# The last stage of an attention and two-MLP kernel written in a fixed order on every engine, with the rooms of its first inputs moved

## The chip, the cores and the metric

The kernel runs on one core of a Trainium2 chip. The metric is the device time of one execution in microseconds (us): the median of several runs. In this text PE is the matrix engine (TensorE) and PEld its weight loads, DVE the VectorE, ACT the ScalarE, POOL the GpSimd, and SP the engine that issues nearly all transfers.

## The reference

Attention over 4 sequences of 576 positions with 8 heads of 64, half of them with a local window of 32, half with a stride of 32; then one MLP with a product, then a second with a gelu. All is in float32.

```python
x = attn_out.transpose(0, 2, 1, 3).reshape(2304, 512)
y = (((x @ w1) * (x @ w2)) @ w3) @ moe_w_out       # 512 -> 1024 -> 512
h = y @ w_in                                       # 512 -> 2048
g = h * (1.0 / (1.0 + np.exp(-1.702 * h)))
return g @ w_out                                   # 2048 -> 512
```

## The kernel before

**Arithmetic.** Every float32 factor is split in a high part (ACT, `split_hi`, L246) and a low part (DVE, `split_lo`, L252: the rest). A product of two factors is three matmuls: high by low, low by high, high by high (`ORDER`). The weights arrive as 64-bit words that ACT and DVE turn into float32 first: two ACT conversions (L1137, L1138) and three DVE steps (L1139 to L1141). The products of the second MLP go by a scheme with seven products for a 2 by 2 block product, so each weight unit is turned into seven combinations of 256 columns.

**Stages.** Three lists of steps are written ahead of the last stage, `steps1`, two called `steps2`, and `steps3`. Each step has a time in units of 12 matmuls of 288 columns, and `written` sorts a list and issues it in that order on PE, DVE, ACT and SP. The batches of attention and of the first MLP run in them. Beside that work the weights of the second MLP are prepared:

- `u_placed`: eight units of `w_in` are converted and stored to `widram` (stage `steps2`; times `UNITS_2`).
- `wo_steps`: eight units of `w_out` are converted, summed into seven combinations, split and stored to `tdram`, high parts by `store(0)` and low parts by `store(1)`. Unit 0 is early (`EARLY_AT`, in the second `steps2`, rooms in pool `cv`). Units 1 to 6 are in `steps3` (`UNIT` apart), unit 7 is late, in the last stage.

`steps3` is the last batch. Its first 8 units (-8 to 0) are the end of the batch before: `y_products` (L1166) with their copies `ysb` (L1174), which go to `ydram`. From 0 on come `pieces(3, hb, m)` (L715): per m two products of 12 matmuls, a copy on ACT (`abf`, L1226), a multiplication on DVE (L1229), and a split into `ab` (L246, L252), and `fourth` (L1350), the last product of the first MLP. Beside it stand `y_load` (L1290), which reads the first 768 rows of y back from `ydram`, and `y_steps` (L1308, L246, L252), which forms seven combinations of y and splits them into `yq`. `y_load(0, 0)` goes into the tile `raw` of pool `cv_a`, `y_load(0, 1)` into that of `cv_b`; the rooms of `steps3` (pools on the right side of the memory) come to lie where pools of the earlier stages lay.

**The last stage** (second MLP) runs over 3 blocks of 768 rows. A block has 8 quads and then 5 sweeps. A quad (`quad`) takes one unit of `w_in`, `hl`: seven products of six matmuls with 384 columns (`product`, L1461) into three PSUM tiles x, y, z, with copies of x and z by ACT (`keep`, L1474: s1, u1, z1), additions by DVE (L1467), gelu by ACT (L1453), differences by DVE (L1470), and a split of two of the results (`split`, tile `sp`). The five results of a quad stay in `parts[i]`. Between the products of quad i stand two pieces (`piece`, L1483: nine matmuls with 256 columns) of quad i - 1. A sweep is eight pieces, one for each `parts[i]`. The pieces read `tdram` factors from a ring of eight rooms (`t_more`, L1442). The factors of a quad come by `w_fetch` (L1327) and are split by `w_split`. The fetch of quad n is issued in quad n - 2, into the tile `x` of `cv_a`.

Unlike the stages before it, this last one isn't written by times: a planner (the scheduler of the tile framework, which reorders instructions of one engine by its own costs) decides the order on each engine. On PE it also takes pieces apart: a few matmuls of one stand between those of a product.

## Time and profile before

| | us |
|---|---|
| median of 3 runs | 818.17 (815.62 to 819.21) |
| the profiled execution, its own time | 817.43 |
| its span, first to last instruction | 815.6 |
| PE busy, share of the span | 780.1, 96% |
| PEld busy | 750.5, 92% |
| DVE busy | 585.6, 72% |
| ACT busy | 484.8, 59% |

Times in the rows are microseconds from the start of the span. An instruction's row has its start, its duration, engine, line, the tiles it writes and reads, their sizes, and in brackets the idle time of the engine before it with what ended that. A row of the timeline may merge several instructions of one kind (x30). The ends of matmuls are modelled, so a bracket on PE leaves out a part of each gap; the distance between starts has all of it. The chain follows the work that ended last back from the end. The last stage begins on PE at about 442 us; 337 to 379 us is the passage from the third to the last batch of the first MLP.

### The profile page before, as it was taken

To read this page: it belongs to the slowest core of one execution; us is meant where nothing else is said; L and a number is where in the kernel's file an instruction comes from. 1 tells how busy PE (TensorE), PEld (TensorE's weight loads), DVE (VectorE), ACT (ScalarE), POOL (GpSimd) and SP (SyncE) were. 2 spreads that over 40 slices of the span, in tenths; PEclk is the share of its full clock that TensorE was granted. 3 is DMA by queue.
4 is the path that set the end of the run, shared out by engine and by line. 5 is a ranking of instruction groups with operands and counts; after the bars stand their busy time and mean duration, and the time that the engine had idled before them with its cause. 6 is when DMAs were issued, how large, how long until landed. Compare 5 with 4: busy or idle time off the path is not lost.

```text
span 815.6 us, 16751 instructions
## 1 busy us (share of the span) xinstructions
PE 780.1 (96%) x6545; PEld 750.5 (92%) x6545; DVE 585.6 (72%) x1248; ACT 484.8 (59%) x1040; POOL 5.8 (1%) x14
## 2 busy tenths in 40 slices
PE   5899999999999999879999998999999999999997
PEld 4889999978999999878999898999999999999997
DVE  4889678788787787837776786885576885667653
ACT  6857655576665464425546665864566764666553
POOL 2000000000000000000000000000000000000000
PEclk9999999999999999989999999999999999999999
DMA  8976555541887553177899876499344489344472
GB/s 264 301 283 235 176 174 179 181 146 39 289 269 264 165 211 129 59 218 222 239 279 296 309 194 227 168 327 333 129 145 154 167 275 314 112 160 147 134 249 83
DMA packets 72063, 168.14 MB, mean 206 GB/s; under 512 B 6321, under 2 KB 45233, under 8 KB 69425
## 3 DMA queue, kind: packets, MB, share of 16 engines
q1 hardware_dynamic: 71840, 167.04, 62.2%
q8 instruction: 51, 0.84, 0.4%
q14 instruction: 28, 0.22, 0.1%
q10 hardware_dynamic: 144, 0.04, 0.0%
HBM read 130.88 MB, written 36.18 MB: 205 GB/s over the span
## 4 chain that ended last, share of the span: by engine, by line
PE 72%; DMA 11%; DVE 8%; ACT 6%; issue 1%; SPq 0%; ACTq 0%; DVEq 0%
PE acc L1483 21%; PE ps L715 18%; PE ps L1461 17%; PE ps L1166 8%; PE acc L1018 3%; DMA x<-widram 2%; PE acc L1350 2%; ACT hl L246 1%; PE sc L532 1%; DMA raw<-in_w 1%; DMA rawx<-in_w 1%; DVE hl L252 1%; DMA tdram<-sums 1%; PE pv L601 1%; DMA abdram<-abf 1%
## 5 line engine op out<-in xcount | busy, mean ns | idle before, releaser
L1483 PE MATMUL acc<-w,sp 128*128 128x256 f32 x1512 | 190.2, 283 | 1.4 <-DVE sp L252 1.1
L1483 PEld LDWEIGHTS acc<-w,sp 128*128 128x128 f32 x1512 | 187.1, 191 | 3.4 <-ACT sp L246 1.7
L1461 PE MATMUL ps<-yq,hl 128*128 128x384 f32 x924 | 171.1, 337 | 3.7 <-ACT s L1474 3.7
L1461 PEld LDWEIGHTS ps<-yq,hl 128*128 128x128 f32 x924 | 158.0, 188 | 7.4 <-ACT s L1474 7.1
L252 DVE TENSOR_TENSOR sp<-part,sp 128x384 fp32r<-128x384 f32 x144 | 77.8, 556 | 54.0 <-ACT sp L246 53.3
L715 PE MATMUL ps<-xah,w 128*128 128x288 f32 x512 | 104.1, 298 | 0.0
L715 PE MATMUL ps<-xbh,w 128*128 128x288 f32 x512 | 102.6, 295 | 0.7 <-DVE w L252 0.7
L246 ACT ACTIVATE sp<-part 128x384 fp32r<-128x384 f32 x144 | 73.7, 525 | 44.9 <-PE acc L1483 43.5
L715 PE MATMUL ps<-xal,w 128*128 128x288 f32 x256 | 77.8, 304 | 7.7 <-ACT ysb L1174 5.1
L1166 PE MATMUL ps<-ab,w 128*128 128x288 f32 x576 | 81.3, 301 | 2.7 <-DVE ab L252 2.6
L715 PEld LDWEIGHTS ps<-xah,w 128*128 128x128 f32 x512 | 83.6, 191 | 0.0
L715 PEld LDWEIGHTS ps<-xbh,w 128*128 128x128 f32 x512 | 81.9, 188 | 1.2 <-DVE w L252 1.2
L1166 PEld LDWEIGHTS ps<-ab,w 128*128 128x128 f32 x576 | 78.8, 191 | 3.8 <-DVE ab L252 2.9
L715 PE MATMUL ps<-xbl,w 128*128 128x288 f32 x256 | 77.2, 301 | 1.7 <-ACT abf L917 1.3
L1453 ACT ACTIVATE part<-part 128x384 f32<-128x384 f32 x72 | 37.3, 524 | 41.3 <-DVE part L1467 40.8
L246 ACT ACTIVATE ab<-abf 128x288 fp32r<-128x288 f32 x64 | 27.6, 440 | 55.3 <-DVE abf L1229 47.6
L715 PEld LDWEIGHTS ps<-xal,w 128*128 128x128 f32 x256 | 49.0, 191 | 9.9 <-ACT ysb L1174 5.7
L252 DVE TENSOR_TENSOR hl<-x,hl 128x1792 fp32r<-128x1792 f32 x21 | 42.5, 2025 | 16.2 <-ACT hl L246 16.1
L715 PEld LDWEIGHTS ps<-xbl,w 128*128 128x128 f32 x256 | 48.0, 188 | 3.2 <-ACT abf L917 1.5
L1018 PE MATMUL acc<-w,w 128*128 128x512 f32 x192 | 45.8, 398 | 0.1
L1470 DVE TENSOR_TENSOR part<-part 128x768 f32<-128x768 f32 (+1 forms) x48 | 36.3, 757 | 11.9 <-ACT part L1453 11.2
L1018 PEld LDWEIGHTS acc<-w,w 128*128 128x128 f32 x192 | 35.9, 188 | 9.3 <-ACT raw L1024 0.8
(180 smaller groups left out, 1079.0 us busy)
## 6 DMA issues: line engine op xcount, KB each, us to landing
w<-tdram SPq DMA_DIRECT2D x84, 512.0 KB, 5.3
x<-widram SPq DMA_DIRECT2D x21, 896.0 KB, 4.6
raw<-in_win SPq DMA_DIRECT2D x8, 1024.0 KB, 5.3
widram<-x SPq DMA_DIRECT2D x8, 896.0 KB, 5.4
raw<-in_wout SPq DMA_DIRECT2D x6, 1024.0 KB, 6.2
tdram<-raw SPq DMA_DIRECT2D x6, 896.0 KB, 5.3
tdram<-sums SPq DMA_DIRECT2D x6, 896.0 KB
raw<-in_w3t SPq DMA_DIRECT2D x10, 512.0 KB, 4.8
```

The source lines that it names most:

```text
L246: nc.scalar.activation(hi, src, AF.Copy)
L252: e.tensor_tensor(lo, src, r(hi), op=ALU.subtract)
L532: nc.tensor.matmul(sc[:nq, g, i * P:i * P + nk], qs[rows, i], ks[rows, i], start=True, stop=True,)
L601: nc.tensor.matmul(pv[rows, h // 2, :nq], L["v"][:nk, h * D:(h + 1) * D], ps[:nk, h * nq:(h + 1) * nq], start=True, stop=True,)
L715: nc.tensor.matmul(ps, ws[a][m // 2][:, at:at + P], xh[c][:, k, cols], start=(k == 0 and (a, c) == ORDER[0]), stop=(k == KC - 1 and (a, c) ...
L1018: nc.tensor.matmul(acc[f], hl[:, a, f * P:(f + 1) * P], wor[c][g], start=(g == 0 and (a, c) == ORDER[0]), stop=(g == MC - 1 and (a, c) == ...
L1166: nc.tensor.matmul(yacc[n], wfs[a][k][:, n * P:(n + 1) * P], hold[s % 2, k][:, c], start=(k == 0 and (a, c) == ORDER[0]), stop=(k == MC - ...
L1350: nc.tensor.matmul(st[0], wfs[a][k][:, n * P:(n + 1) * P], hold[hb, k][:, c], start=(k == 0 and (a, c) == ORDER[0]), stop=(k == MC - 1 and ...
L1453: nc.scalar.activation(dst, src, AF.Gelu_apprx_sigmoid)
L1461: nc.tensor.matmul(ps, w[a][:, f * 256 + kk * P:f * 256 + (kk + 1) * P], yq[:, b, kk, c], start=(first and kk == 0 and (a, c) == ORDER[0]) ...
L1470: nc.vector.tensor_tensor(dst, x, y, op=ALU.subtract)
L1483: nc.tensor.matmul(to, g[:, a, t * P:(t + 1) * P], t3[:, i % 2, c], start=(opens and i == 0 and n == 0 and t % 2 == 0), stop=(i == NU - 1 ...
```

## The change

- The last stage is written as the others are, in a list `steps4` with times in us (`do`), so the order on PE, DVE, ACT and SP is fixed. A product counts 1.05, a piece 1.07, a quad 9.49. `Quad`, `Split`, `Factors`, `Out` and `after` hold the steps. The arithmetic is the same.
- In the last quad of a block the piece of its first result stands ahead of its last product, and the piece of its last result stands behind the first two pieces of the first sweep. Copies and additions of the accumulators are placed one by one.
- The factors of quads 2 and 3 are fetched at the stage's start into the low half of their own split tiles; later ones three quads ahead, by turns into the tiles `x` and `raw` of `cv_a`. The split of the factors is cut: high part, first 1024 columns of the low part, the rest. A block's first factors are split in the sweeps before it.
- The late unit of `w_out` is spread over quads 1 to 5, and its high part goes to `parts[6]` and not to the raw room.
- Pool `cv_a` is opened ahead of `yc`, so both lie elsewhere on the right side.
- In the stages before: unit 7 of `w_in` one unit of time earlier, the early unit of `w_out` 2.2 earlier, the y steps and the units of `w_out` of the last batch 0.8 later, and the units 7.2 instead of 7.3 apart.

The diff, cut to its core (helpers that only change their names, and the copies and additions of the accumulators, are left out):

```diff
--- before.py
+++ after.py
...
-UNITS_2 = ((4, 6.4), (5, 15.6), (6, 24.2), (7, 32.8))
+UNITS_2 = ((4, 6.4), (5, 15.6), (6, 24.2), (7, 31.8))
...
-EARLY_AT = 37.8
+EARLY_AT = 35.6
...
-    def wo_steps(u, raw, room):
+    def wo_steps(u, raw, room, high_room=None):
         view = lambda t: raw().bitcast(t).rearrange("p (n t) -> p n t", t=2)
-        hi = lambda: raw().bitcast(F32R)[:, :7 * 256]
+        hi = lambda: (high_room or raw)().bitcast(F32R)[:, :7 * 256]
...
+    cv_a = pool("cva", stack=right1, side="right")
     yc = pool("yc", stack=right1, side="right")
-    cv_a = pool("cva", stack=right1, side="right")
     cv_b = pool("cvb", stack=right2, side="right")
...
-    def w_fetch(n, room=None):
+    def w_fetch(n, room):
         if n < NB * NU:
-            if room is not None:
-                x = room
-            elif n == 2:
-                x = p2.tile([P, 2, 7 * 256], F32, tag="hl", name="lent")[:, 0]
-            else:
-                x = cv_a.tile([P, 2 * CW2], F32, tag="x", name="x")[:, 256:]
-            nc.sync.dma_start(x, widram[n % NU])
-            wq[n] = x
...
-    def w_split(n):
-        if n < NB * NU:
-            t = (p2 if n % 2 else cv_a).tile([P, 2, 7 * 256], F32R, tag="hl", name="hl")
-            split_hi(t[:, 0], wq[n])
-            split_lo(t[:, 1], wq[n], t[:, 0])
-            wq[n] = t[:, 0], t[:, 1]
...
+            nc.sync.dma_start(room, widram[n % NU])
+            wq[n] = room
...
-    for kk, at in ((0, -4.4), (1, -1.2)):
+    for kk, at in ((0, -3.6), (1, -0.4)):
...
-    UNIT = 7.3
+    UNIT = 7.2
     for u in range(1, NU):
-        at = 1.8 + UNIT * (u - 1)
-        steps3.append((-1.4 if u == 1 else 1.55 + 0.1 * u if u < 4 else at - 2 * UNIT + 0.2, lambda u=u: wo_load(u)))
+        at = 2.6 + UNIT * (u - 1)
+        steps3.append((-0.6 if u == 1 else 2.35 + 0.1 * u if u < 4 else at - 2 * UNIT + 0.2, lambda u=u: wo_load(u)))
         if u < NU - 1:
             steps3 += [(at + g, f) for g, f in wo_steps(u, lambda u=u: todo3[u], lambda u=u: sums[:, u % 2])]
...
-    def t_more():
-        owed[0] += 1
-        t_load()
-
...
+    def t_more(k=1):
+        owed[0] += k
+        while owed[0] and flown[0] < len(flow) and not (held[0] and flow[flown[0]][2] == NU // 2 - 1):
             owed[0] -= 1
+            n = flown[0]
             b, j, c = flow[n]
             t = ring[n % len(ring)]
             nc.sync.dma_start(r(t), tdram[j, c].rearrange("p u s n -> p (u s n)"))
             factor[flow[n]] = t.rearrange("p (u s n) -> p u s n", u=2, s=2)
             flown[0] += 1
...
+    def t_release():
+        held[0] = False
+        t_more(0)
...
+    class Factors:
+
+        def __init__(self, n):
+            self.n = n
+
+        def fetch_in_place(self):
+            self.t = (p2 if self.n % 2 else cv_a).tile([P, 2, 7 * 256], F32R, tag="hl", name="hl")
+            w_fetch(self.n, r(self.t[:, 1]))
+
+        def fetch(self):
+            tag, typ, w = (("x", F32, 2 * CW2), ("raw", I64, CW2))[self.n % 2]
+            w_fetch(self.n, cv_a.tile([P, w], typ, tag=tag, name="fetched").bitcast(F32)[:, :7 * 256])
+
+        def hi(self):
+            self.raw = wq.pop(self.n)
+            if not hasattr(self, "t"):
+                self.t = (p2 if self.n % 2 else cv_a).tile([P, 2, 7 * 256], F32R, tag="hl", name="hl")
+            split_hi(self.t[:, 0], self.raw)
+            wq[self.n] = self.t[:, 0], self.t[:, 1]
+
+        def lo(self, lo, hi):
+            c = slice(lo, hi)
+            split_lo(self.t[:, 1, c], self.raw[:, c], self.t[:, 0, c])
...
+    class Quad:
+
+        def __init__(self, b, i, X, Y, pre):
+            at = b * BLOCK + i * QUAD
...
+            D(0, begin)
+            D(0.01, prod, "x", 0, 0, True, False)
+            D(1.05, prod, "y", 1, 1)
+            D(2.1, prod, "x", 4, 4, False, False)
+            D(3.15, prod, "z", 3, 3, True, False)
+            if pre:
+                D(4.2, piece, X, b, B11, i - 1, pre.c11, True)
+            D(5.27, prod, "x", 5, 5, False, False)
+            D(6.32, prod, "z", 6, 2, False)
+            if pre:
+                D(7.37, piece, Y, b, B21, i - 1, pre.a12, True)
+            if pre and i % 2 == 0:
+                D(8.5, t_more, 2)
+            end = 8.44
+            if i == NU - 1:
+                D(8.4, piece, X, b, B11, i, self.c11, True)
+                end += PC
+            D(end, prod, "x", 2, 6, False)
+            end += MM
+            g = AF.Gelu_apprx_sigmoid
+            D(1.1, keep, "s1", "x")
+            D(2.9, act, st(2), st(2), g)
+            D(3.4, keep, "u1", "x")
+            D(4.25, keep, "z1", "z")
+            D(4.8, self.c11.hi)
+            D(7.05, act, st(0), st(0), g)
+            D(8.65, act, st(1), st(1), g)
+            D(end + 0.05, last)
+            D(end + 0.6, self.a12.hi)
+            D(2.85, dve, st(2), get("y"), get("s1"), ALU.add)
+            D(5.4, self.c11.lo)
+            D(6.4, dve, st(0), get("x"), get("z1"), ALU.add)
+            D(8.2, dve, st(1), get("z"), get("u1"), ALU.add)
+            D(9.7, dve, st(3, 5), st(0, 2), st(1, 3))
+            D(10.2, dve, st(1), st(0), st(4))
+            turn = i == NU - 1
+            D(11.5 if turn else 10.3, dve, st(2), get("a12"), st(1))
+            D(11.4 if turn else 10.4, self.a12.lo)
+
+    W = [Factors(n) for n in range(NB * NU)]
+
+    def w_steps(n, at, late=0):
+        do(at + 5.3, W[n].hi)
+        do(at + 7.0, W[n].lo, 0, 1024)
+        do(at + 8.75, W[n].lo, 1024, 7 * 256)
+
+    def open_parts():
+        slots_s[0].close()
+        where = pool("parts4", reuse_waits="tile")
+        more_parts(where)
+        more["y"] = where.tile([P, 2 * BT], F32, name="second_raw")
...
+    def after(b, q, X, Y):
+        A0 = b * BLOCK + NU * QUAD + PC
...
+        order = [(n, i) for n in range(5) for i in range(NU)]
+        pos = [s if s < 2 else s + 1 for s in range(len(order))]
+        sp = [Split(lambda n=n, i=i: parts[i][:, SWEEP[n][1]]) for n, i in order]
+        D(PC * 2, piece, Y, b, B21, NU - 1, q.a12, True)
+        for s, (n, i) in enumerate(order):
+            D(PC * pos[s] + 0.01, piece, (X, Y)[n % 2], b, SWEEP[n][0], i, sp[s], n == 1)
+            if i % 2:
+                D(PC * (pos[s] + 1) + 0.02, t_more)
+            if s < 3:
+                D(-QUAD - PC + 5.3 + 0.05 * s, sp[s].hi)
+                D(-QUAD - PC + (7.0, 8.3, 8.4)[s], sp[s].lo)
+            else:
+                D(PC * (pos[s] - 3) + 0.1, sp[s].hi)
+                D(PC * (pos[s] - 3) + 0.65, sp[s].lo)
+        D(PC * 3 + 0.02, t_more, 2)
...
+            D(-MM + 0.05 + 0.05 * n, c11.copy, X, n)
+            D(3.3 + 1.1 * n, c11.add, Y, n, c11)
...
+        if b + 1 < NB:
+            n = (b + 1) * NU
+            do(A0 + 2.7, W[n].hi)
+            D(5.3, W[n].lo, 0, 1024)
+            D(7.0, W[n].lo, 1024, 7 * 256)
+            D(-NU * QUAD + 4.5 * QUAD, y_fetch, b + 1, 0)
+            D(-PC - QUAD + 0.4, y_fetch, b + 1, 1)
+            for kk, at in ((0, 8.0), (1, 17.5)):
+                gaps = (0.3, 1.4, 2.4, 3.5, 3.7, 4.6, 4.8, 5.8, 6.0, 7.5)
+                for m, g in enumerate(gaps):
+                    D(at + g, lambda m=m, kk=kk, b=b: more_steps(b, kk)[m]())
+            D(27.5, W[n + 1].fetch)
+            D(28.5, W[n + 2].fetch)
...
+    todo3_hi = lambda: parts[NU - 2].rearrange("p n t -> p (n t)")
+    todo3_lo = lambda: parts[NU - 1].rearrange("p n t -> p (n t)")
+    late = [f for _, f in wo_steps(NU - 1, lambda: todo3[NU - 1], todo3_lo, todo3_hi)]
...
+    for f, (i, t) in zip(late, (
+        (1, 1.7), (2, 1.7), (2, 3.5), (2, 3.6), (3, 3.5), (3, 3.6), (4, 3.5), (4, 3.55), (4, 3.6),
+        (4, 9.2), (5, 1.7), (5, 3.5), (5, 3.55), (5, 3.6), (5, 5.9),
+    )):
+        do(i * QUAD + t, f)
+    do(5 * QUAD + 6, t_release)
+    do(2 * QUAD - 0.01, open_parts)
+
+    do(-0.9, t_more, 2)
+    do(-0.8, W[2].fetch_in_place)
+    do(-0.7, t_more, 2)
+    do(-0.6, W[3].fetch_in_place)
+    do(-0.5, t_more, 4)
     for b in range(NB):
...
-                g = quad(b, i, *steps)
-                n = b * NU + i + 2
-                if n > 3:
-                    w_fetch(n)
-                if i < NU - 1:
-                    w_split(n)
...
-                if i == 4 and b + 1 < NB:
-                    ys = [y_load(b + 1, 0), y_load(b + 1, 1, lambda: second_raw)]
...
-                steps[0]()
-                ob, o = copied(X)
-                steps[1]()
-                nexts = [split(parts[n][:, 1]) for n in range(3)]
...
+        for i in range(NU):
+            q = Quad(b, i, X, Y, q)
+            n = b * NU + i
+            at = b * BLOCK + i * QUAD
+            if i < NU - 1 and n > 0:
+                w_steps(n + 1, at)
+            if n == 2:
+                do(at + QUAD + 5.35, W[n + 3].fetch)
+            elif 0 < n < NB * NU - 3 and i < NU - 2:
+                do(at + 9.8, W[n + 3].fetch)
+        after(b, q, X, Y)
+    written(steps4)
```

## Rows read from the trace of the kernel before

**Rows 1.** Stretches: us, busy PE, PEld, DVE, ACT, POOL (instructions), clock, DMA share, GB/s.

```profile
336.70:379.00 42.30, 32.60 (x207) 30.86 (x205) 25.48 (x40) 15.67 (x26) 0.00 (x0) 0.88 0.52 170
379.00:442.20 63.20, 62.57 (x468) 62.34 (x469) 45.78 (x74) 33.00 (x54) 0.00 (x0) 1.00 0.95 265
...
586.13:595.68 9.55, 9.55 (x62) 9.39 (x61) 6.62 (x9) 5.96 (x11) 0.00 (x0) 1.00 0.33 109
```

**Rows 2.** Chain that ended last: start us, us, engine, tile, line, instructions; unbroken matmuls.

```profile
390.31 12.80 PE acc L1350 x96
...
586.29 5.33 PE ps L1461 x30
...
591.62 1.07 PE acc L1483 x9
```

**Rows 3.** Timeline of PE, 337 to 363 us: start, us, instruction, count [idle before <-releaser].

```profile
342.29 11.78 PE L1166 MATMUL ps<-ab,w 128*128 128x288 f32 x75 [2.63 <-DVE ab L252]
...
359.11 0.40 PE L715 MATMUL ps<-xal,w 128*128 128x288 f32 x1 [3.45 <-ACT ysb L1174]
...
362.77 0.61 PE L715 MATMUL ps<-xal,w 128*128 128x288 f32 x1 [1.65 <-ACT ysb L1174]
```

**Rows 4.** Chain, 346 to 358 us: a store and the load behind it.

```profile
346.23 7.29 DMA tdram<-x
...
353.66 4.47 DMA raw<-ydram
```

**Rows 5.** Timeline of ACT, 358 us.

```profile
358.23 0.52 ACT L246 ACTIVATE yq<-raw 128x384 fp32r<-128x384 f32 x1 [13.02 <-DMA raw<-ydram]
358.66 0.39 ACT L1174 ACTIVATE ysb<-ps 128x288 f32<-128x288 f32 x1
```

**Rows 6.** Timeline of DVE, 337 to 365 us.

```profile
337.38 0.70 DVE L1139 TENSOR_SCALAR x<-x 128x1024 int32<-128x1024 int32 x1 [1.40 <-ACT x L1138]
...
341.79 0.45 DVE L252 TENSOR_TENSOR ab<-abf,ab 128x288 fp32r<-128x288 f32 x1
342.15 0.88 DVE L1126 TENSOR_TENSOR x<-x 128x256 f32<-128x256 f32 x2
344.11 2.10 DVE L252 TENSOR_TENSOR x<-x,raw 128x896 fp32r<-128x896 f32 x2 [1.08 <-ACT raw L246]
...
358.34 0.56 DVE L1308 TENSOR_TENSOR x<-raw 128x384 f32<-128x384 f32 x1 [12.14 <-DMA raw<-ydram]
...
364.24 0.56 DVE L1308 TENSOR_TENSOR x<-raw 128x384 f32<-128x384 f32 x1
```

**Rows 7.** Waits of PE, 445 to 530 us: us in total, times, longest.

```profile
PE ps L1461 <- ACT s L1474: 3.7, 3, 2.5
...
PE ps L1461 <- ACT u L1474: 1.1, 1, 1.1
```

**Rows 8.** Timeline of ACT and of PE, 496 to 498 us.

```profile
495.98 1.70 ACT L246 ACTIVATE hl<-x 128x1792 fp32r<-128x1792 f32 x1 [2.45 <-DMA x<-widram]
497.58 0.47 ACT L1474 ACTIVATE s<-ps 128x384 f32<-128x384 f32 x1
...
498.11 1.31 PE L1461 MATMUL ps<-yq,hl 128*128 128x384 f32 x6 [2.54 <-ACT s L1474]
```

**Rows 9.** Chain, 485 to 496 us: a low part and the load behind it.

```profile
485.05 2.04 DVE hl L252
...
487.10 8.86 DMA x<-widram
```

**Rows 10.** Timeline of PE at the second turn: first and last row, 31 matmuls between.

```profile
643.45 1.21 PE L1461 MATMUL ps<-yq,hl 128*128 128x384 f32 x6
...
649.36 5.90 PE L1483 MATMUL acc<-w,sp 128*128 128x256 f32 x47 [0.44 <-DVE sp L252]
```

**Rows 11.** Chain at the second turn.

```profile
646.80 2.03 DVE hl L252
```

**Rows 12.** Timeline of ACT, 439 us.

```profile
439.33 1.71 ACT L246 ACTIVATE w<-w 128x1792 fp32r<-128x1792 f32 x1 [1.53 <-DMA w<-widram]
```

More of the change, by code (lines that the diff above doesn't have):

```diff
@@ L1412, in body @@
     parts = []
-    def late_steps():
-        room = lambda: parts[NU - 1].rearrange("p n t -> p (n t)")
-        return [f for _, f in wo_steps(NU - 1, lambda: todo3[NU - 1], room)]
     def more_parts(where):
@@ L1497, in copied @@
-    def copied(acc):
-        return read_out(lambda d, s, c: nc.scalar.activation(d, s, AF.Copy), acc)
-    def summed(acc, o):
-        return read_out(lambda d, s, c: add(d, s, o[:, c]), acc)[0]
-    def put(b, right, d, ob):
-        c0 = b * BT + right * HT
-        nc.sync.dma_start(out[c0:c0 + HT, d * 256:d * 256 + 256].rearrange("(t p) n -> p t n", p=P), ob)
-    def quad(b, i, one, two):
-        w = wq.pop(b * NU + i)
-        y, z, x = (mm.tile([P, HT], F32, tag="mm", name="ps") for _ in range(3))
-        st = parts[i]
-        product(x, w, 0, 0, True, False)
-        s1 = keep("s1", x)
-        product(y, w, 1, 1)
-        add(st[:, 2], y, s1)
-        product(x, w, 4, 4, False, False)
-        u1 = keep("u1", x)
-        product(z, w, 3, 3, True, False)
-        z1 = keep("z1", z, 1)
-        gelu(st[:, 2], st[:, 2])
-        first_ = split(st[:, 2])
-        one()
-        product(x, w, 5, 5, False, False)
-        add(st[:, 0], x, z1)
-        gelu(st[:, 0], st[:, 0])
-        product(z, w, 6, 2, False)
-        add(st[:, 1], z, u1)
-        gelu(st[:, 1], st[:, 1])
-        two()
-        product(x, w, 2, 6, False)
-        a12 = f32("a12")
-        gelu(a12, x)
-        second = split(a12)
-        minus(st[:, 3:5], st[:, 0:2], st[:, 1:3])
-        minus(st[:, 1], st[:, 0], st[:, 4])
-        minus(st[:, 2], a12, st[:, 1])
-        return first_, second
@@ new lines, in body, with room, copy, add @@
+    WIDE = (slice(0, 512), slice(512, 768))
+    class Out:
+        def room(self):
+            self.t = p2.tile([P, HT // P, 256], F32, tag="ob", name="ob", bufs=3)
+            self.o = self.t.rearrange("p t n -> p (t n)")
+        def copy(self, acc, n):
+            if n == 0:
+                self.room()
+            nc.scalar.activation(self.o[:, WIDE[n]], acc[n][:, :768 - 512 if n else 512], AF.Copy)
+        def add(self, acc, n, other):
+            if n == 0 and other is not self:
+                self.room()
+            nc.vector.tensor_tensor(self.o[:, WIDE[n]], acc[n][:, :768 - 512 if n else 512], other.o[:, WIDE[n]], op=ALU.add)
+        def put(self, b, right, d):
+            c0 = b * BT + right * HT
+            nc.sync.dma_start(out[c0:c0 + HT, d * 256:d * 256 + 256].rearrange("(t p) n -> p t n", p=P), self.t)
@@ new lines, in body, with accs @@
+    do(5 * QUAD + 6, t_release)
[5 more added lines that the diff above has]
+    do(-0.5, t_more, 4)
+    for b in range(NB):
+        X, Y = [None] * 2, [None] * 2
+        def accs(X=X, Y=Y):
+            for t in (X, Y):
+                t[:] = [accp.tile([P, 512], F32, tag="acc", name="acc") for _ in range(2)]
+        do(b * BLOCK + QUAD + 4.1, accs)
+        q = None
+        for i in range(NU):
+            q = Quad(b, i, X, Y, q)
+            n = b * NU + i
+            at = b * BLOCK + i * QUAD
[6 more added lines that the diff above has]
+        after(b, q, X, Y)
```

142 lines of the change are left out of this document (60 added, 82 removed).

## The prediction

> **What bounds the kernel now.** TensorE (PE) does. The page gives it 96% of the span, but the ends of matmuls are modelled, so I don't go by that share. I go by starts: how many matmuls a stretch holds, what that many take where nothing holds PE, and what is left over. The view of stretches comes first [rows 1]; the clean spacings come from the chain [rows 2]: 12.80/96 = 0.133 us for a matmul of 288 columns, 5.33/30 = 0.178 for one of 384 in the last stage, 1.07/9 = 0.119 for one of 256. In 336.7:379 there are 207 matmuls worth 207 x 0.133 = 27.6 us in 42.3: 14.7 us are lost. In 379:442.2 there are 468, worth 62.4 of 63.2: nearly nothing. So the bound of the whole is PE's own work, and what a change of order can give back lies in a few stretches: the change of batch at 337 to 379, the opening of the last stage, and the turns between its blocks. In between, a quad of the last stage (42 products, 18 pieces) takes 42 x 0.178 + 18 x 0.119 = 9.6 us of PE, and one of the second block has PE full for all its 9.55 us, DVE busy for 6.62 and ACT for 5.96 [rows 1]: there no order improves anything.
>
> Second view: PE's timeline, with the releaser in brackets [rows 3]. The reader is to see three waits of 2.63, 3.45 and 1.65 us. The first is for a low part that VectorE (DVE) writes, the others for copies by ScalarE (ACT). In the last row a matmul takes 0.61 us where the one before took 0.40: the clock has fallen, and the stretch's mean is 0.88 [rows 1], a mix of 2.4 and 1.2 GHz. The three waits make 7.7 of the 14.7; the other 7.0 are the lower clock and several small waits behind them.
>
> Third view: the chain shows why ACT was late [rows 4]. The store of the first unit's low part runs from 346.23 and takes 7.29 us; the load of y is issued at 353.66, 0.14 us behind its end. It waits for that store because y's room lies on the first unit's. ACT stands 13.02 us for y, and the copy that PE wants (ysb) comes right behind at 358.66 [rows 5]: a strict queue. DVE stands 12.14 us as well [rows 6].
>
> **Part 1, the change of batch.** The two right-hand pools change places, so y's room lies on attention tiles that are done with long before; only yq now lies on the first unit's rooms, and nothing writes it before y is there. Then y's load needs no landing, only its turn on SP behind the two stores. The early unit stands 2.2 steps earlier. A step is 12 matmuls x 0.133 = 1.6 us, so 3.5 us; in the rows DVE is full, so I take 3.0: the second store goes at 343.3. The load alone takes 4.47 us [rows 4]. It lands at 347.8 if it isn't slowed by the stores, at 343.3 + 7.3 + 4.5 = 355.1 if it runs wholly behind them. I take 352, since two stores share the engines with it.
>
> What gets worse: the early unit's steps now stand ahead of the last block's product and low part on DVE. Ahead of that low part (341.79) come two low halves (2.10 us) and a pair of sums (0.88); the 1.40 us in which DVE stood for ACT's conversion goes, as that conversion is earlier too [rows 6]. So 2.10 + 0.9 - 1.4 = 1.6 later: PE's first wait grows from 2.63 to 4.2 us. Bounds: 2.6 if DVE catches up, 5.6 if nothing of the 3.0 is hidden.
>
> Before, the new batch started where the 75 matmuls of rows 3 end, at 342.29 + 11.6 = 353.9; now at about 353.9 + 1.6 = 355.5. The first y step and the next one on ACT no longer precede the copies that PE wants at once: y's first part moves 0.8 step later, behind the second ysb copy. With y at 352, DVE is done with the first half of y at 357.9 (364.24 - 358.34 = 5.9 us) and gets to the first product of the batch after some 4 of the other half's 5.9 us, at 362 [rows 6]; PE needs that bank five steps in, at 355.5 + 8 = 363.5. DVE then has a conversion between the products, so I leave 1.1 us of small waits. The waits of 3.45 and 1.65 go. Of the other 7.0 I let about a third, 2.4, stay: one fall of the clock after the one long wait. What stays: 4.2 + 1.1 + 2.4 = 7.7; gain 14.7 - 7.7 = 7.0. With y at 355.1 the products come 3 us later and the gain is 4.
>
> **Part 2, the last stage's first block.** Between 445 and 530 PE waits 3.7 + 1.1 = 4.8 us, all for ACT's copies s and u [rows 7]. The worst: ACT stands 2.45 us for a load of second-layer factors, splits it for 1.70, and only then writes s, which PE awaits for 2.54 [rows 8]. That load ran from 487.10 to 495.96 [rows 9]. In the new order loads are issued up to three quads ahead, into two rooms in turn, two of them in place; the split is placed at 5.3 us of each quad, when its load has had a whole quad (9.55 us, against the 8.86 of that load). ACT then never waits at the head of its queue. The late unit's 15 steps lie one to four to a quad; DVE has 6.62 us of its own in a quad's 9.55 [rows 1], and the heaviest quad adds two low halves, 2.10 [rows 6], so it fits. Its high part now goes out from parts[6], issued at 3.55 us of quad 5 and to be gone when quad 6 writes there 8.9 us later; such a store took 7.29 [rows 4], so 1.6 are left. All 4.8 come back, 5.0 with the start-up of each wait; I leave 0.5 for new ones, as the first quad's waits (low part of the first factors) stay.
>
> At the head of SP's queue the in-place load waits until the last unit's store has landed, and the ring's loads wait behind it. They are wanted a quad and more later; cover about 4 us; if it were gone, each us would be a us.
>
> **Part 3, the turns.** From 643.45 to 649.36 there are 18 products and 13 pieces, 18 x 0.178 + 13 x 0.119 = 4.7 us in 5.9: 1.2 lost, of which the row names 0.44 [rows 10]. Ahead of the low part that PE awaits, DVE has split the next factors for 2.03 [rows 11]. The new order puts the piece of the last quad's late split behind two pieces of the sweep (2.1 us, against gelu, split and subtraction of some 1.6) and moves the factors' split away. Two such turns and a last one half as large: 3.0, of which I leave 0.4. Gain 2.6.
>
> **Part 4, the seam.** The units of the last batch move with UNIT to 7.2 and a start of 2.6: the fifth's stores, behind which the first factors' load queues, are 0.4 step = 0.6 us later to PE. ACT already waits 1.53 us for that load before PE's first product of the stage [rows 12], so this counts: -0.6.
>
> **Sum.** 7.0 + (5.0 - 0.5) + 2.6 - 0.6 = 13.5. The profiled execution took 817.43 us (span 815.6, 1.8 around it), 0.7 under the median of the runs. 817.43 - 13.5 = 803.9; I say 804.
>
> **Rivals.**
> A: y still waits for the store, because a room is freed with its whole pool. For: the two pools still touch by a few kB. Against: the wait ended 0.14 us behind one store [rows 4], which a wait for one tile gives as well. The store is 3 us earlier all the same, so y lands at 355.1, part 1 gives 4: 807.
>
> B: the first block's waits are a matter of room, not of order. For: that load started at 487.10, when DVE had just done with its room (485.05 + 2.04) [rows 9], and the waits for s come three times, a quad apart [rows 7]. They would stay: 804 + 4.5 = 808.5. The Trainium skill (Perfetto Trace Analysis, Optimization Strategy) says that a gap which repeats on the engine that should be full can mean too little memory for the next tile. By that rule alone the order would give nothing here and the time would be 808.5; the trace agrees in that the load is issued when the room falls free, but the change adds a second room.
>
> C, slower than before: ACT in every quad. PE's third product needs s; between the first product's end and that lies one product, 6 x 0.178 = 1.07 us; s takes 0.47, and the end of six products lies 1.31 - 1.07 = 0.24 behind their last slot [rows 8], so 0.36 are to spare. Ahead of s in the fixed order stand gelu and split of the quad before, of about its own length, 0.5 each, and in the old order whatever was ready went first. If a late input makes ACT slip by d in each quad, PE loses d - 0.36 in each of 24. It decides at d = 0.36; d = 0.95 costs 14 us and undoes all (818); two steps late by their own length, d = 1.2, cost 20 and give 824.
>
> D: the early unit's earlier place costs PE the full 5.6, and the clock stays low as long as before: part 1 then gives 14.7 - 5.6 - 1.1 - 7.0 = 1.0 in place of 7.0: 810.
>
> **How the numbers follow.** Forecast (800 to 806) 0.55; better than 800, with y at 347.8 and the first wait at 2.6, 0.10; A 0.11; B 0.09; C 0.09, of which 0.05 is slower than before and 0.03 near it; D 0.06. The likeliest gives 804. The range 799 to 811 takes in A, B and D and most of what is better and leaves out C: about 0.83. A measurement here tells some 0.5% (4 us) from no change: faster 0.88, same 0.07, slower 0.05.
>
> **What would show it.** Right: y's load issued before 346, landing near 352; ACT's wait for it under 7 us; PE's waits in the change of batch one of about 4 us and small ones; no wait of PE for s or u above 0.5 us in the first block; turns under 0.3 us; the last stage's quads still 9.55 us. Wrong: y issued behind the store's end (A), ACT waiting for factors at the head of its queue (B), a third product that waits in every quad (C), a first wait over 5 us (D). A fall of the clock in the last stage would make everything wrong.

## The result, and the profile after

The changed kernel takes 805.06 us (median; 804.05 to 805.41) beside 818.69 of the kernel before: a ratio of 0.9836, interval 0.9805 to 0.9867. Run again later it took 805.77 (802.39 to 807.98) beside 817.41, ratio 0.9847 (0.9812 to 0.9882). The forecast was 804, range 799 to 811, faster. The profiled execution took 805.01, its span 803.2.

The time was right; the terms were not all. To see where the time went I use a table that can be made from any two traces of this kernel. The record has 6545 matmuls in every run here, and up to number 4024 they come in one order, so the time between two numbers belongs to one stage. In us, worked out from the starts of PE's matmuls (the last column ends at the last matmul):

```
kernel                 opening   change of batch   seam        rest of last stage
                       0-3350    3350-4024         4024-4066   4066-6544
before                 336.31    105.80             8.79       360.31
after                  333.36    101.65            12.46       351.32
after, run again       334.37    100.88             9.96       351.20
```

The seam is the passage from the last batch of the first MLP to the last stage. So between the two profiles the change of batch gave 4.15 (4.92 in the second look), the seam took 3.67 (1.17), and the last stage gave 8.99 (9.11). Another 2.95 (1.94) lie in the opening: at matmul 1016, ahead of everything that the edits move, 2.89 (2.18) are there already.

First the stretches, as in [rows 1] (us, busy PE, PEld, DVE, ACT, POOL with instructions, clock, DMA share, GB/s); the kernel after:

```profile
333.80:376.00 42.20, 34.59 (x236) 32.58 (x236) 26.36 (x45) 17.11 (x29) 0.00 (x0) 0.96 0.58 184
376.00:435.10 59.10, 58.63 (x439) 58.22 (x437) 42.12 (x69) 28.64 (x48) 0.00 (x0) 1.00 0.97 265
435.10:442.60 7.50, 4.70 (x18) 4.24 (x16) 4.61 (x3) 6.07 (x9) 0.00 (x0) 0.78 0.96 296
452.95:462.38 9.43, 9.43 (x62) 9.43 (x61) 8.33 (x12) 6.98 (x13) 0.00 (x0) 1.00 0.43 173
447.50:559.10 111.60, 111.60 (x800) 111.55 (x799) 86.39 (x143) 72.09 (x130) 0.00 (x0) 1.00 0.71 256
```

The reader is to see three things. The change of batch holds 236 matmuls in 42.2 us where it held 207 in 42.3: better, but 42.2 - 236 x 0.133 = 10.8 us are still lost. The third row is the seam: 18 matmuls in 7.5 us with the clock at 0.78. Before, one wait of 0.57 us for a low part stood there (first row below). The last two rows are the surprise: a quad takes 9.43 us, not 9.55, and from 447.5 to 559.1 the profile shows no idle time of PE. The same 800 matmuls took this in the kernel before (second row):

```profile
443.15 7.04 PE L1461 MATMUL ps<-yq,w 128*128 128x384 f32 x35 [0.57 <-DVE w L252]
...
450.90:570.90 120.00, 114.58 (x800) 112.00 (x800) 90.26 (x140) 74.80 (x132) 0.00 (x0) 1.00 0.75 257
```

Second, y. SP's timeline of the kernel after (start, us, line, transfer), VectorE's row for y's first step, ScalarE's for its first copy:

```profile
340.43 0.36 SPq L1121 DMA_DIRECT2D tdram<-x  x1
348.22 0.87 SPq L1290 DMA_DIRECT2D raw<-ydram  x2
...
353.06 0.56 DVE L1308 TENSOR_TENSOR x<-raw 128x384 f32<-128x384 f32 x1 [12.29 <-DMA raw<-ydram]
...
353.22 1.26 ACT L246 ACTIVATE yq<-raw 128x384 fp32r<-128x384 f32 x2 [6.80 <-DMA raw<-ydram]
```

The chain has the store at 340.43 for 7.66 us, to 348.09. The load of y is issued 0.13 us behind that, as in [rows 4], so y still waits for the store. What did change is ACT's order: it stands 6.80 us for y, no longer 13.02 [rows 5], as two copies that PE wants now precede.

Third, the seam (chain, ACT, PE of the kernel after), to be held against [rows 12]:

```profile
421.67 12.99 DMA w<-widram
...
434.74 1.70 ACT L246 ACTIVATE w<-w 128x1792 fp32r<-128x1792 f32 x1 [4.10 <-DMA w<-widram]
...
436.49 0.44 PE L1479 MATMUL ps<-yq,w 128*128 128x384 f32 x1 [1.18 <-ACT w L246]
438.55 4.79 PE L1479 MATMUL ps<-yq,w 128*128 128x384 f32 x17 [1.62 <-DVE w L252]
```

ACT waits 4.10 us for the first factors where it waited 1.53, and now PE waits behind it, twice.

### The profile page after: what moved, and what is told of

It is laid out like the page before. It is cut to its first block, busy times and chain, and to the rows that moved or that the text cites. A ratio compares the mean times of both kernels' runs of the same rounds, so it can differ in the third digit from the quotient of the medians.

```text
span 803.2 us, 16781 instructions
## 1 busy us (share of the span) xinstructions
PE 775.2 (97%) x6545; PEld 749.8 (93%) x6545; DVE 580.2 (72%) x1270; ACT 480.3 (60%) x1040; POOL 5.8 (1%) x14
## 4 chain that ended last, share of the span: by engine, by line
PE 74%; DMA 9%; DVE 8%; ACT 6%; issue 2%; SPq 0%; ACTq 0%; DVEq 0%
PE acc L1490 22%; PE ps L1479 21%; PE ps L715 16%; PE ps L1166 8%; PE acc L1018 3%; DMA raw<-in_w 2%; DMA w<-widram 2%; PE sc L532 1%; DMA ql<-in_ql 1%; DMA vl<-in_vl 1%; PE pv L601 1%; DVE w L252 1%; DMA tdram<-x 1%; DVE sums L1126 1%; ACT w L246 1%
## 5 line engine op out<-in xcount | busy, mean ns | idle before, releaser
L1490 PE MATMUL acc<-w,sp 128*128 128x256 f32 x1512 | 188.2, 282 | 0.0
L1479 PE MATMUL ps<-yq,hl 128*128 128x384 f32 x924 | 169.1, 335 | 0.9 <-DVE hl L252 0.6
L252 DVE TENSOR_TENSOR sp<-part,sp 128x384 fp32r<-128x384 f32 x144 | 75.1, 552 | 57.7 <-ACT sp L246 57.5
L715 PE MATMUL ps<-xah,w 128*128 128x288 f32 x512 | 102.3, 294 | 0.0
L246 ACT ACTIVATE sp<-part 128x384 fp32r<-128x384 f32 x144 | 69.2, 519 | 21.3 <-PE acc L1490 19.3
L252 DVE TENSOR_TENSOR hl<-fetched,hl 128x1024 fp32r<-128x1024 f32 (+1 forms) x40 | 43.3, 1083 | 1.7 <-ACT hl L246 1.7
L246 ACT ACTIVATE w<-xw 128x512 fp32r<-128x512 f32 (+1 forms) x30 | 23.2, 773 | 29.0 <-DVE xw L808 28.7
```

What stands on the lines that cost most here:

```text
L246: nc.scalar.activation(hi, src, AF.Copy)
L252: e.tensor_tensor(lo, src, r(hi), op=ALU.subtract)
L715: nc.tensor.matmul(ps, ws[a][m // 2][:, at:at + P], xh[c][:, k, cols], start=(k == 0 and (a, c) == ORDER[0]), stop=(k == KC - 1 and (a, c) ...
L1479: nc.tensor.matmul(ps, w[a][:, f * 256 + kk * P:f * 256 + (kk + 1) * P], yq[:, b, kk, c], start=(first and kk == 0 and (a, c) == ORDER[0]) ...
L1490: nc.tensor.matmul(to, g.t[:, a, t * P:(t + 1) * P], t3[:, i % 2, c], start=(opens and i == 0 and n == 0 and t % 2 == 0), stop=(i == NU - ...
```

## The experiments

Each kernel was run beside the kernel before, whose median lay between 817.39 and 817.80; kernels of one group shared a chip. Their stages, from one profile each, by matmul number as above:

```
kernel                                  time     opening  batch    seam    rest
after, run again                        805.77   334.37   100.88    9.96   351.20
old front, new last stage               807.51   333.99   105.89    9.27   351.30
new front, old last stage               814.44   333.68   100.86   10.94   360.42
pools back                              804.61   336.06   101.05    9.66   351.19
y's room apart                          805.00   335.65   100.60   12.27   351.19
y's first half ahead of the stores      800.97   332.81    97.85   12.78   351.18
first factors earlier                   803.51   335.68   100.99    8.92   351.28
room apart + first factors earlier      802.43   333.98   100.62    8.31   351.25
quads in the old order                  810.36   335.86   100.88   10.28   356.08
y first + first factors earlier         798.44   334.00    97.71    9.34   351.24
the same, low halves behind             799.46   334.55    98.78    8.50   351.17
```

**The two halves of the change.** The kernel after with all that stands ahead of the last stage as before (the edit, condensed; the units' loads move with `at`):

```diff
-UNITS_2 = (..., (7, 31.8))   EARLY_AT = 35.6   cv_a, then yc
+UNITS_2 = (..., (7, 32.8))   EARLY_AT = 37.8   yc, then cv_a
-y's steps at -3.6, -0.4      UNIT = 7.2        at = 2.6 + UNIT * (u - 1)
+y's steps at -4.4, -1.2      UNIT = 7.3        at = 1.8 + UNIT * (u - 1)
```

> The last stage as in the changed kernel, all that stands ahead of it (early unit, order of the pools, places of y's steps and of the units) as in the kernel before. From the two traces I book 9.3 us to the last stage (368.97 us from its first product to its last matmul before, 362.30 after, and some 2.6 to 3.9 of it hidden by a slower seam that is now counted apart). Theory (the stage's gain is its own, the seam's loss comes from the units' later places): 818.7 - 9.3 = 809.4, ACT's wait for the first factors back to about 1.5 us, quads at 9.43 us. Rival (the stage gives what was forecast, 4.5 + 2.6 = 7.1, and the quads' 0.12 us are a matter of the front): 811.6 with quads at 9.55. Rival (the slow seam belongs to the new stage): ACT waits over 3 us for the first factors, and about 813. If the 2.9 us of the opening, which no edit touches, show here too, each of these is 2.9 less.

And the kernel before with the same lines turned the other way:

> The other half alone: early unit, order of the pools, places of y's steps and of the last batch's units as in the changed kernel, the last stage as in the kernel before. Theory (y still waits for the store, part 1 gives 4, the later units cost the seam 3.9): 818.7 - 4 + 3.9 = 818.6, no change. Rival (the forecast's terms, 7.0 - 0.6): 812.3. Rival (the seam's loss belongs to the new stage): 814.7. The opening's 2.9 us would come off each.

Measured: 807.51 and 814.44 beside 817.8, ratios 0.987 (0.9848 to 0.9891) and 0.9952 (0.9936 to 0.9968). The gains of 10.3 and 3.4 add to 13.7; the whole change gave 13.6 and 11.6. The last stage's rest is 351.30 with the old front and 360.42 with the new front and the old stage: its 9 us are its own. The seam takes 9.27 with the old front and the new stage, and 10.94 the other way round, and the first factors' load says which half loses it: in the kernel before and with the old front it lands 2.9 and 3.0 us ahead of matmul 4024, in the seven profiles with the later units and this load in its place 0.0 to 1.9 us ahead. So the later units, not the new stage, lose it. The time of the second kernel alone would not have told: 814.44 lies at the 814.7 of the rival that gives the seam's loss to the new stage, and only the stages (batch 4.9 less, seam 2.2 more, opening 2.6 less) speak against it.

**The swap of the pools.** (A room is the place of a tile in the core's memory, a pool a group of rooms.)

```diff
-    cv_a = pool("cva", ...)
-    yc = pool("yc", ...)
+    yc = pool("yc", ...)
+    cv_a = pool("cva", ...)
```

> The changed kernel with the two right-hand pools in the order of before (yc ahead of cva), nothing else moved. Theory (y waits for the store with either order, since in either one the pool of y's room touches the pool of the first unit's rooms): y issued at the store's end as in the changed kernel, no stage different, 805 to 806. Rival (the order of the pools gives something after all): y's load or VectorE's first step for y later than in the changed kernel by 2 us and more, 808.

Measured 804.61, and by its own clock y was issued 350.30 - 336.06 = 14.24 us behind matmul 3350, where the changed kernel has 348.22 - 333.36 = 14.86. The swap does nothing: the store ends at 350.17, and with either order the issue stands 0.13 us behind that end. (That a room waits for every pool that its pool touches fits this and the next run, but no run shows the rule itself.)

**y's room in a pool of its own**, opened first, so that only the attention's tiles lie under it:

```diff
+    cv_r = pool("cvr", stack=right1, side="right")
     cv_a = pool("cva", ...)
-    ... cv_a.tile([P, CW2], I64, tag="raw", ...)     # y_load, rooms[0], Factors.fetch
+    ... cv_r.tile([P, CW2], I64, tag="raw", ...)
```

> The changed kernel with y's room (the tag raw of the pool cva) in a pool of its own, opened first, so that it touches only the attention's tiles; nothing else of the order changes. Theory (a room waits for all pools that its own pool touches; cva still overlaps the pool of the first unit's rooms by some kB): y's load is issued at about 341 to 345 in place of 348.2, lands at 348 to 351 in place of 353.05, and the change of batch gives back 2 to 3 us more: 802.5. Rival (y isn't what PE waits for there, but the early unit's steps ahead of the last batch's low parts on VectorE): the load is issued earlier and the time stays 805. Rival (the load waits for something other than that pool): issue still at 348, 805.

Measured 805.00, no difference. SP and DVE of that kernel:

```profile
342.72 0.36 SPq L1121 DMA_DIRECT2D tdram<-x  x1
343.19 2.46 SPq L1291 DMA_DIRECT2D raw<-ydram  x2
...
354.42 0.56 DVE L1309 TENSOR_TENSOR x<-raw 128x384 f32<-128x384 f32 x1 [11.36 <-DMA raw<-ydram]
```

The load is issued 0.47 us behind the store's issue and no longer at its end: by the stage's clock 7.54 us behind matmul 3350 instead of 14.86. But VectorE starts on y 18.77 us behind it, where the changed kernel has 19.70, its second run 19.08, and the other kernels with the wait 18.7 to 18.9. Issued seven us earlier, y was there no earlier beyond this spread. My theory fell as stated: the wait was real, and taking it away alone gave nothing.

**y's load ahead of the stores on SP's queue.** The rooms are those of the kernel just shown; the first half of y goes first, then the stores of the early unit (condensed):

```diff
-    steps2 += [(EARLY_AT + g, f) for g, f in wo_steps(0, ...)]
+    early_unit = wo_steps(0, ...)
+    steps2 += [... all of early_unit but its two stores]
     written(steps2)
+    written([(0, y_first_load), (5.35, store of the high part), (6.4, store of the low part)])
```

> As the kernel with y's room apart, and the first half of y's load goes onto SP's queue ahead of the two stores of the early unit instead of behind them. In that kernel the load was issued 7.3 us earlier by the stage's own clock and landed only 0.9 us earlier, 11.2 us behind its issue. Theory (the stores' bytes share the engines with it, so the place in the queue and not the wait sets the landing): the first half lands 4 to 5 us behind its issue, near 348; VectorE's first step for y is then set by the stores' landing, since its outputs lie on the rooms that they read, some 2 us earlier than before; PE gains 0.5 to 1.5 us over the kernel with y's room apart. Rival (the landing isn't what PE waits for): y earlier, and PE's time from the last product of the old batch to the fourth of the new one the same within 0.3 us.

Measured 800.97 (800.10 to 802.49) beside 805.77 of the changed kernel. The change of batch takes 97.85 us, 2.75 less than with y's room apart, more than I had expected. SP, DVE and the waits of PE (us in total, times, longest; 333 to 380 us):

```profile
330.80 0.38 SPq L1284 DMA_DIRECT2D raw<-ydram  x1
338.24 0.37 SPq L1121 DMA_DIRECT2D tdram<-raw  x1
339.90 0.36 SPq L1121 DMA_DIRECT2D tdram<-x  x1
...
348.82 0.56 DVE L1319 TENSOR_TENSOR x<-raw 128x384 f32<-128x384 f32 x1 [8.58 <-DMA tdram<-x]
...
PE ps L1166 <- DVE ab L252: 3.9, 2, 2.9
```

DVE now waits for the store, under which its outputs lie, and starts 16.01 us behind matmul 3350 instead of 18.7 to 19.7. Of PE's waits in that stretch only the first is left; in the changed kernel (332 to 380 us) three more groups stand there:

```profile
PE ps L1166 <- DVE ab L252: 3.8, 2, 2.9
PE ps L715 <- DVE abf L1229: 1.7, 2, 1.5
PE ps L715 <- ACT abf L1226: 1.4, 2, 1.1
PE ps L715 <- ACT ysb L1174: 0.6, 2, 0.4
```

So y's landing does hold PE, and here it is the place in the queue that sets it, not the wait.

**The first factors' load earlier.** One DMA moved on SP's queue:

```diff
-            (40.05 + 0.1 * n, lambda n=n, lo=lo: w_fetch(n, r(lo))),
+            ((31.55, 40.15)[n], lambda n=n, lo=lo: w_fetch(n, r(lo))),
```

> The changed kernel with one DMA moved: the load of the first second-layer factors goes onto SP's queue ahead of the last unit's load and of the fourth-from-last pair of stores instead of behind them (step 31.55 in place of 40.05). Theory (the seam's stall, 4.10 us of ACT and then 1.62 us of PE behind VectorE and a spell at half the clock, comes from that load alone, which was issued at 421.67 and landed at 434.66): the first product follows the last matmul of the earlier stage without a stall, 805.1 - 4 = 801. Rival (the DMA engines are full, 0.97 busy from 376 to 435, so what the load gains the stores lose, and the ring's loads are late in its place): 805. Between the two: 803.

Measured 803.51, against the two medians of the changed kernel 1.6 and 2.3 less. The changed kernel was not run in this group; its 805.06 and 805.77 come from two others. By number the seam takes 8.92 where it took 12.46 and 9.96. SP, ACT and PE of that kernel:

```profile
411.22 1.38 SPq L1321 DMA_DIRECT2D w<-widram  x1
...
432.19 1.69 ACT L246 ACTIVATE w<-w 128x1792 fp32r<-128x1792 f32 x1
...
427.73 9.23 PE L1333 MATMUL acc<-ab,w 128*128 128x288 f32 x68
436.80 5.55 PE L1479 MATMUL ps<-yq,w 128*128 128x384 f32 x30
```

ACT finds the first factors there and PE goes from the old stage into the new one without a wait; only behind its first 30 matmuls does it wait, 0.77 us for ACT's copy z. The load is the cause. How much it costs differs by execution of one program: in the second run of the changed kernel it took 11.63 us and not 12.98, and ACT stood 2.75 us for it, not 4.10.

**Both edits**, y's room apart and the first factors earlier:

> The two edits that were tried singly, together: y's room in a pool of its own, and the load of the first second-layer factors ahead of the last unit's load. By matmul number the first gave 1.1 us in the change of batch and the second 0.6 there and 3.5 at the seam. Theory (they add): 4.5 under the changed kernel run beside it, about 801. Rival (the same DMA engines, so the one takes from the other): 3.5 or less.

Measured 802.43, 3.3 below the changed kernel beside it; the seam is at 8.31 and the batch at 100.62, the same as with the room apart. That is inside the rival's 3.5 or less, not the theory's 4.5, but no sharing is needed for it: the seam's part is there, and the room's part is nothing.

**The quads in the order that the planner had chosen before.**

```diff
-        do(at + 5.3, W[n].hi)
+        do(at + 0.08, W[n].hi)
-            D(2.1, prod, "x", 4, ...)    D(3.15, prod, "z", 3, ...)
+            D(2.1, prod, "z", 3, ...)    D(3.15, prod, "x", 4, ...)
```

(The copies u and z change places with them.)

> The changed kernel with the quads' order as the planner had it in the kernel before: on ScalarE the high part of the next factors stands between the last gelu of a quad and the copy s of the next one, and on PE the third and fourth product of a quad change places. 20 of the 24 quads are touched. Theory (a quad took 9.55 us before because s came 0.1 us late behind that split, and this is where the 9.43 come from): quads at 9.55 again, 20 x 0.12 = 2.4 us slower than the changed kernel run beside it, no other stage moved. Rival (the 0.12 comes from the order of products and pieces elsewhere in the quad): quads at 9.43 and no difference; or, if the margin is thinner than it was, 0.3 and more per quad, 6 us.

Measured 810.36, 4.6 over the changed kernel; the last stage's rest takes 4.88 more. The quads of the second and third block are at 9.55 again (starts of every 42nd product), and these blocks take 120.77 and 120.75 us where they took 119.91 and 119.88. In the second block five quads take 0.12 more each, and the first two together 0.2. ACT of that kernel at one quad:

```profile
589.65 0.49 ACT L1546 ACTIVATE a<-ps 128x384 f32<-128x384 f32 x1 [0.44 <-PE ps L1479]
590.03 1.70 ACT L246 ACTIVATE hl<-fetched 128x1792 fp32r<-128x1792 f32 x1
591.63 0.52 ACT L246 ACTIVATE sp<-a 128x384 fp32r<-128x384 f32 x1
592.04 0.48 ACT L1542 ACTIVATE s<-ps 128x384 f32<-128x384 f32 x1
```

The 1.70 us of the split stand ahead of s, which ends at 592.52; the product that needs it starts at 592.57. (The edit moves the split and exchanges two products at once; what either does alone was not run.) Of the other 3 us, 2.1 are one quad of the first block, of 11.60 us: there the split itself waits for a load, at the head of ACT's queue, and PE waits for s behind it:

```profile
449.74 1.70 ACT L246 ACTIVATE hl<-hl 128x1792 fp32r<-128x1792 f32 x1 [1.85 <-DMA w<-tdram]
...
452.28 1.33 PE L1479 MATMUL ps<-yq,w 128*128 128x384 f32 x6 [1.80 <-ACT s L1542]
```

That is a wait as in [rows 8], made by the order alone, with the new rooms in place.

**A second look at the changed kernel.**

> The changed kernel once more, as it is, for its times beside the next three on the same chip, and for a second look at the opening, which no edit touches: up to matmul 1016 of the record the changed kernel's profile is 2.9 us ahead of the one of before, and two of the four kernels run since are 2.2 behind it with the same code there. Theory (the opening differs from execution to execution): the median lies at 805 to 807 with a spread of some 2 us, and the spans differ by what the opening took. Rival (the opening belongs to the build): 805.0 with matmul 1016 at 61.4 again.

Matmul 1016 came at 62.09 us, where the first profile has 61.38 and the one of before 64.27. No edit of any kernel here touches what precedes it, and over the 13 profiles it comes between 60.77 and 64.27, matmul 3350 between 332.81 and 336.31; the profile of before is the latest of all. But these are 12 programs, and the two profiles of one program differ by 0.71 and 1.01 us at these two matmuls, so whether the 3.5 us belong to the execution or to the build is not shown. The median of 805.77 is the theory's; the spread of the times, 5.6 us, is wider than its 2.

**The version that beats both: y first and the first factors earlier.**

> The kernel with the first half of y's load ahead of the stores, and the load of the first second-layer factors ahead of the last unit's load as well. Singly, by matmul number, the first leaves 97.85 us from matmul 3350 to 4024 (the changed kernel 101.65 and, run again, 100.88) but its seam, matmul 4024 to 4066, takes 12.78; the second takes the seam to 8.92. Theory (they add, since one is about the queue at 340 us and the other about the queue at 415): seam under 9 us, 801.0 - 3.9 = 797.1. Rival (the earlier batch meets the late loads all the same, the engines are full): seam over 10.5, 799 or more.

Measured 798.44 (798.14 to 801.98) beside 817.39, ratio 0.9782 (0.9759 to 0.9805); the theory had 797.1, the rival 799 or more. The seam is at 9.34, between the two expectations; in place of the factors PE now waits 1.35 us for ACT's copy z, whose room lies under a store of ysb:

```profile
438.59 1.31 PE L1491 MATMUL ps<-yq,w 128*128 128x384 f32 x6 [1.35 <-ACT z L1554]
```

**The early unit's last splits behind PE's low part.** In the kernel just shown, steps 9 to 14 of the early unit go behind the last low part that PE needs in the old batch:

```diff
-    behind = (12, 14)
+    behind = (9, 10, 11, 12, 13, 14)
```

> As the one before it, and the last four splits of the early unit (two high halves on ScalarE, two low ones on VectorE) go behind the last low part that PE waits for in the old batch, with the stores that read them. Theory (PE's wait of 2.9 us there is VectorE's and ScalarE's work on the early unit ahead of that low part, as the forecast had it): the low part comes 2.2 us earlier, the spell at half the clock behind it gets shorter by 1 to 2 us, the stores and with them VectorE's first step for y come 1 us later and take back at most 1; together 2 to 3 us: 794.5. Rival (what PE gains at the old batch's end it waits for at the new one's start, since y's steps are the next thing that is late): 797, no difference.

Measured 799.46, no better: the rival holds. Its timeline of PE:

```profile
339.82 10.27 PE L1166 MATMUL ps<-ab,w 128*128 128x288 f32 x75 [0.68 <-DVE ab L252]
354.18 0.40 PE L715 MATMUL ps<-xal,w 128*128 128x288 f32 x1 [0.93 <-ACT ysb L1174]
```

The wait of 2.86 us is down to 0.68, and from matmul 3350 to 3450 the kernel gains 3.7 us; from 3450 to 3600 it loses 4.8, since the stores and with them y's steps come later (ACT now stands 7.26 us in front of yq for the store).

## Why the prediction came out as it did

The time was right, in part by luck, since misses of both signs cancelled. Part 1 was to give 7.0 and gave 4.15 (4.92 in the second look). Parts 2 and 3 were to give 7.1 and gave 8.99 (9.11). Part 4 was to cost 0.6 and cost 3.67 (1.17). And 2.95 (1.94) lie in the opening, which no part names and whose cause stays open.

**Part 1, 7.0 forecast, 4.2 and 4.9 measured.** The first wait was right: 1.6 later was the step, and matmuls 3350 to 3375 take 7.88 us where they took 6.22. The step that failed is "y's load needs no landing, only its turn on SP". Rival A's wait happened, and its price was right: 4 (its reason, a room freed with its whole pool, only fits). It had 0.11, on the argument that a wait that ends 0.14 us behind one store fits a wait for one tile as well. It did fit, and decided nothing. Behind it a second step was wrong: the landing at "352, since two stores share the engines". With the wait really gone, y was there 11.2 us behind its issue, close to the forecast's other end, "wholly behind them" (7.3 + 4.5). What the forecast had priced exists: with y ahead of the stores the change of batch takes 97.85, 7.95 less than before. The clock's 2.4 us: matmuls 3375 to 3400 take 4.45 and 5.88 where a clean run of 25 takes 3.33, so 1.1 and 2.6 in two executions.

**Part 2, 4.5 forecast; it gave more.** From number 4066 to the end of the first block the changed kernel is 8.4 us faster (120.0 against 111.6 in the two rows above). Starts of PE's matmuls give what had been lost there: 5.5 in four waits for s and u ([rows 7] have 4.8), 0.9 at the first turn, 0.1 in each quad, and small ones. No load is awaited at the head of ACT's queue any more, as the forecast said. Rival B, that these waits are a matter of room and that order gives nothing, falls with the quads in the old order: the rooms are the new ones, and one large wait for s and the 0.1 us in each quad are back. That is 4.9 us of the last stage's 9; no run puts the old rooms back under the new order, so what the rooms have in the rest is not shown. The Trainium skill (Perfetto Trace Analysis, Optimization Strategy) says that such a repeating gap can mean a lack of room; no run here bears this out as the sole cause, and order alone brings 1.80 us of it back.

**Part 3, 2.6 forecast.** The first turn's 0.9 came, inside the 8.4. The second and third block together gave only 0.97 - 0.40 = 0.57, although their quads gave 1.7. A wait for the split of factors did not go: it moved from the turn to the start of the next block's second quad, which takes 10.46 us and so loses 1.0 each time:

```profile
567.28 2.18 PE L1479 MATMUL ps<-yq,hl 128*128 128x384 f32 x11 [0.30 <-DVE hl L252]
569.62 2.37 PE L1479 MATMUL ps<-yq,hl 128*128 128x384 f32 x12 [0.16 <-ACT s L1542]
```

The first quad of a block has no pieces and takes 7.53 us, but the split of the second quad's factors is placed in it at 5.3 to 8.75 us, as in a full quad; its first low part ends at 567.23 and PE goes on at 567.28. So what the second and third turn gained was lost there: "moves the factors' split away" was costed at nothing without a look at where the next split falls.

**"Quads still 9.55".** Wrong, to the good side: 9.43. I took 42 products and 18 pieces at spacings read from a chain, got 9.6 and called the quad full; the chain's 5.33 for 30 products held the 0.1 us of wait for s. Rival C, ACT late with s in every quad, was already there in the kernel before, by 0.1 us. The margin of 0.36 us that C was given was worked out for the new order, and there it holds.

**Part 4, -0.6 forecast, -3.7 and -1.2 measured.** The mechanism was named (the load queues behind the fifth unit's stores) and sized as a shift of 0.6 us. Ahead of matmul 4024 the load is issued 14.6 us in the kernel before and 13.3 and 13.4 in the changed one, so 1.2 later and not 0.6; it lands 2.9 ahead before, 0.4 and 1.7 after. And in the first profile the cost was more than the shift: with ACT's wait 2.6 us longer PE waits for the high part, then for the low part, and then runs at half the clock (18 matmuls, clock 0.78 in the row above), 3.67 in all. In the second ACT's wait is 1.2 us longer, PE waits for the low part alone, the clock stays whole, and the seam costs 1.17.

**The chances.** Of the points named as right or wrong, y behind the store's end, quads at 9.43 and PE's wait at the seam went against the forecast; ACT under 7 us for y, the first wait near 4, no wait for s or u in the first block, and turns under 0.3 went with it.

## To carry to other kernels

A load that waits for a store to land need not be early when the wait is gone: ask what stands ahead of it in the queue and move the load itself; here the place in the queue was worth 3 us and the wait alone nothing. Before calling a repeated stretch full, subtract clean spacings taken between waits, since a wait of 0.1 us in each repeat hides in a mean. And compare stages by instruction number across several executions: here the opening, the same code in all, differed by up to 3.5 us between profiles.

## What the runs showed of the hardware

The half clock behind a stall differs from execution to execution of one program. Stretches of the changed kernel (first profile, from PE's restart), of its second run, and of the last experiment:

```profile
340.80:344.00 3.20, 3.17 (x14) 3.18 (x15) 0.00 (x0) 0.41 (x1) 0.00 (x0) 0.54 1.09 272
344.00:348.00 4.00, 4.00 (x32) 4.00 (x32) 0.00 (x0) 0.41 (x1) 0.00 (x0) 1.00 0.54 151
...
341.80:344.00 2.20, 2.16 (x9) 2.16 (x10) 0.00 (x0) 0.41 (x1) 0.00 (x0) 0.50 1.10 250
344.00:348.00 4.00, 4.00 (x19) 4.00 (x19) 0.00 (x0) 0.00 (x0) 0.00 (x0) 0.50 0.87 231
...
340.00:344.00 4.00, 4.00 (x31) 4.00 (x32) 2.09 (x2) 1.53 (x4) 0.00 (x0) 1.00 0.56 158
```

In the first two, PE had waited 0.98 and 2.87 us (2.86 in the second run) with three matmuls between:

```profile
337.29 0.67 PE L1166 MATMUL ps<-ab,w 128*128 128x288 f32 x3 [0.98 <-DVE ab L252]
340.83 11.55 PE L1166 MATMUL ps<-ab,w 128*128 128x288 f32 x75 [2.87 <-DVE ab L252]
```

Behind these waits the granted clock is 1.2 of 2.4 GHz for some 3 us in one execution and over 6 in the other. In the last PE had waited 0.98 and 0.68 us, and the clock stayed whole. In this kernel the landing of a load followed what stood ahead of it on the queue: the same load of y took 4.8 us from issue to VectorE's first step when issued behind the stores' end, and 11.2 when issued 0.5 us behind their issue.
